# Four rearrangements in a fused state-space and GeGLU kernel: token halves at the start, earlier x, paired gate products, coefficients on GpSimd

## The chip, the cores and the metric

The kernel runs on one core of one Trainium2 chip. The metric is the device time of one execution in microseconds (us). Each change was timed in the same rounds as the kernel before and is given with a 95% interval.

Five engines matter. TensorE (PE in the profile) multiplies matrices, VectorE (DVE) does element-wise work and scans, ScalarE (ACT) does activations and copies, GpSimd (POOL) does small vector work, and SyncE (SP) issues most transfers. The issue queue of SyncE is SPq.

## The reference, cut to what matters

```python
xn = _layernorm(x)                                     # x: [1, 2048, 512]
# A: diagonal complex recurrence, state size 512
h = Lam_bar * h + Bu[t]                                # t = 0 .. 2047, Bu = xn @ B_bar^T
s = 2 * Re(hseq @ Cmat^T) + xn * Dskip
# B: gated feed-forward, F = 1376
g = silu((gelu(xn @ w_gate) * (xn @ w_up)) @ w_down)
out = x + s * g
```

## The kernel before

Tokens are worked in four slabs of 512 (`s`), the 1376 hidden features in eleven tiles (`j`). Per tile, TensorE makes a gate and an up product, ScalarE brings both out of PSUM (gelu, copy), and VectorE multiplies them. The y blocks (output of the recurrence) of slab s-1 are placed between tiles of slab s, and so is the layer norm of slab s+1.

The start normalises slab 0 on VectorE, in two pairs of tiles of 128 tokens, and transposes on TensorE:

```python
dummies(9); ...; dummies(5)               # warm-up matmuls, result unused
...
xs = [norm0(0), norm0(1)]                 # VectorE: xn = (x - mean) * rstd
tps = [t_xn0(0, xs[0]), t_xn0(1, xs[1])]  # TensorE transposes
xnT_out(nc.vector, 0, tps[0])
xnT_out(nc.scalar, 1, tps[1])
xs += [norm0(2), norm0(3)]
second_half()                             # the same for tiles 2 and 3
... # angles: thn, ang, kr on VectorE; sines sh, ch on ScalarE
nc.gpsimd.tensor_copy(out=v4(sa[:]), in_=sh[...])     # wide copy, 128 x 2048
```

The gate and up products of one tile, with the multiplication. `dve(ready, cost, f)` puts an instruction into VectorE's program; a clock of estimated times in the builder decides which waiting instructions go in front of it, so another cost or time changes VectorE's order:

```python
def ffn(s, j, at):
    ... # g_ps = wg tile x xnT, u_ps = wu tile x xnT, 512 columns each
    gt = work.tile([P, TS], BF16, name="gt", tag="gt", bufs=4)
    ACT(out=gt[:fs], in_=g_ps[:fs, :], func=AF.Gelu_apprx_tanh)
    ub = work.tile([P, TS], BF16, name="ub", tag="ub", bufs=4)
    ACT(out=ub[:fs], in_=u_ps[:fs, :], func=AF.Copy)
    dve(now() + 0.9, 0.34, lambda: TT(out=at[:fs, j, :], in0=gt[:fs], in1=ub[:fs], op=ALU.mult))
```

For slabs 2 and 3 the layer norm is made while the slab before is multiplied. ScalarE sums x and its square, seven small operations on GpSimd, one after the other, make the scale `rs` and the bias `nb` of all four tiles, ScalarE normalises, and a transposing transfer from SyncE lays the tile down as `xnT`.

```python
def ln_small(s):
    G = nc.gpsimd
    mean, var = sx[:, s, 0, :], sx[:, s, 1, :]                 # [128, 4] each
    G.tensor_scalar(out=mean, in0=mean, scalar1=1.0 / D, scalar2=None, op0=ALU.mult)
    G.tensor_tensor(out=mq[:, s, :], in0=mean, in1=mean, op=ALU.mult)
    G.tensor_scalar(out=var, in0=var, scalar1=1.0 / D, scalar2=EPS, op0=ALU.mult, op1=ALU.add)
    G.tensor_tensor(out=var, in0=var, in1=mq[:, s, :], op=ALU.subtract)
    G.tensor_tensor(out=rs[:, s, :], in0=var, in1=mhalf[:], op=ALU.pow)
    G.tensor_tensor(out=nb[:, s, :], in0=mean, in1=rs[:, s, :], op=ALU.mult)
    G.tensor_scalar(out=nb[:, s, :], in0=nb[:, s, :], scalar1=-1.0, scalar2=None, op0=ALU.mult)

def ln_out(s, m):
    ACT(out=xn[:], in_=x_tok[:, s * M + m, :], func=AF.Identity, scale=rs[...], bias=nb[...])
    nc.sync.dma_start_transpose(out=xnT[:, :, c0 : c0 + P], in_=xn[:])
```

## Time and profile before

| | before |
|---|---|
| median of the runs | 188.41 us (188.31 to 188.55) |
| span of the profiled core | 186.4 us |
| TensorE busy | 179.5 us, 96% |
| VectorE busy | 155.3 us, 83% |
| GpSimd busy | 16.8 us, 9% |

TensorE sets the time: it is never long without work, and what another engine does counts only where TensorE then waits. A line of the timeline gives start, duration, engine, source line, operation, output<-inputs, shapes and, in brackets, how long the engine had been idle and what released it. For TensorE the bracket counts from the modelled end of the matmul before and comes out about 0.16 us smaller than the delay; a delay of 0.2 us or less shows none. TensorE's timeline, kernel before, at the first product and at the only gap in mid-kernel:

```profile
9.19 1.02 PE L425 MATMUL g_ps<-xnT,wg 128*128 128x512 bf16 x4 [0.69 <-ACT xnT L202]
...
62.97 1.68 PE L460 MATMUL y_ps<-C,hst 128*128 128x512 bf16 x6 [0.50 <-DVE hst L363]
```

The bracket at the y block is that for the first half of hst; with a shorter wait for the second half, inside the group, the block loses 0.89 us.

GpSimd's timeline, kernel before: the wide copy of the start, and the small statistics of slab 2 (made during slab 1):

```profile
10.27 1.89 POOL L245 COPY sa<-sh 128x2048 bf16<-128x2048 bf16 x1 [0.29 <-ACT sh L228]
...
63.62 0.45 POOL L520 TENSOR_SCALAR sx<-sx 128x4 f32<-128x4 f32 x1 [45.96 <-ACT junk L515]
64.15 0.20 POOL L521 TENSOR_TENSOR mq<-sx 128x4 f32<-128x4 f32 x1
64.44 0.20 POOL L522 TENSOR_SCALAR sx<-sx 128x4 f32<-128x4 f32 x1
64.72 0.20 POOL L523 TENSOR_TENSOR sx<-sx,mq 128x4 f32<-128x4 f32 x1
...
67.00 0.28 POOL L526 TENSOR_SCALAR nb<-nb 128x4 f32<-128x4 f32 x1
```

The copy starts after VectorE's normalisation is over (second pair from 7.32 to 8.05 us). The seven small operations take 67.28 - 63.62 = 3.7 us, four of them 0.2 to 0.3 us each. VectorE stands idle during the three of 0.20 us (from 63.99 to 65.30 us), as its timeline of the same kernel shows; whether this is why they are short, e5 bears on below:

```profile
65.30 0.43 DVE L438 TENSOR_TENSOR at<-gt,ub 128x512 bf16<-128x512 bf16 x1 [1.31 <-ACT ub L437]
```

ScalarE needs their result for the four normalisations. The waits of ScalarE, kernel before (total, times, longest):

```profile
ACT xn L530 <- POOL nb L526: 3.8, 2, 2.7
```

### The profile page before, as it was taken

The page shows a single profiled execution, that of the slowest core. Times are in us where ns is not written, and L with a number is a line of the kernel's source. Part 1 is how long each engine was busy: PE and PEld are TensorE (multiplying, and loading weights), DVE is VectorE, ACT ScalarE, POOL GpSimd, SP SyncE. Part 2 cuts the span into 40 slices and gives each one's busy share as a digit, 9 for nine tenths or more (in the row PEclk, how much of TensorE's full clock was granted, in tenths as well). Part 3 has the DMA queues.
Part 4 walks back from the last instruction along what each step waited for, and adds up shares of the span by engine and source line. Part 5 has one row for each costly group of instructions (what it writes and reads, how often), then busy time and mean ns, then how long its engine had stood idle before and what let it go on. Part 6 is the DMA issues. An engine that isn't in the chain of part 4 may idle for free.

```text
span 186.4 us, 2533 instructions
## 1 busy us (share of the span) xinstructions
PE 179.5 (96%) x887; PEld 84.2 (45%) x887; DVE 155.3 (83%) x266; ACT 115.3 (62%) x208; POOL 16.8 (9%) x35
## 2 busy tenths in 40 slices
PE   7699999999999899999999999999999999999992
PEld 2344444444444344544444444544444444554452
DVE  4948999999977799999999999999999999532034
ACT  3289996677799979257259949747428733451210
POOL 3653000000000230000000080000000000000000
PEclk9999999999999999999999999999999999999999
DMA  5994924896000016200000003310000000000001
GB/s 147 336 306 105 223 49 92 221 250 203 0 0 0 0 24 91 58 28 28 0 0 5 2 0 77 91 30 29 0 0 0 0 4 28 28 30 28 32 28 57
DMA packets 24444, 12.26 MB, mean 66 GB/s; under 512 B 15760, under 2 KB 24432, under 8 KB 24432
## 3 DMA queue, kind: packets, MB, share of 16 engines
q1 hardware_dynamic: 24256, 12.03, 25.2%
q8 instruction: 7, 0.11, 0.3%
q10 hardware_dynamic: 176, 0.07, 0.1%
q14 instruction: 5, 0.04, 0.1%
HBM read 6.33 MB, written 2.10 MB: 45 GB/s over the span
## 4 chain that ended last, share of the span: by engine, by line
PE 88%; ACT 5%; DVE 4%; DMA 1%; issue 1%; ACTq 0%
PE f_ps L445 20%; PE g_ps L425 18%; PE up_ps L430 18%; PE u_ps L343 15%; PE y_ps L460 14%; PE y_ps L465 2%; ACT junk L515 1%; DVE st L154 1%; DMA x_tok<-in_A_x_dram 1%; PE y_ps L493 1%; ACT gt L435 1%; ACT ub L437 1%; ACT L435 1%; DVE qq L359 1%; PE tp L174 1%
## 5 line engine op out<-in xcount | busy, mean ns | idle before, releaser
L425 PE MATMUL g_ps<-xnT,wg 128*128 128x512 bf16 (+1 forms) x176 | 45.2, 379 | 0.7 <-ACT xnT L202 0.7
L430 PE MATMUL up_ps<-xnT,wu 128*128 128x512 bf16 (+1 forms) x176 | 45.2, 379 | 0.0
L445 PE MATMUL f_ps<-wd,at 128*128 128x512 bf16 (+1 forms) x176 | 38.7, 379 | 0.0
L435 ACT ACTIVATE gt<-g_ps 128x512 bf16<-128x512 f32 (+1 forms) x44 | 26.4, 600 | 11.1 <-PE g_ps L425 8.6
L389 DVE TENSOR_TENSOR_SCAN Ft<-rho,it,Wt 128x512 bf16<-128x512 f32 x24 | 30.1, 1274 | 0.0
L437 ACT ACTIVATE ub<-up_ps 128x512 bf16<-128x512 f32 (+1 forms) x44 | 26.5, 602 | 5.1 <-PE up_ps L430 4.9
L460 PE MATMUL y_ps<-C,hst 128*128 128x512 bf16 x120 | 28.7, 379 | 0.5 <-DVE hst L363 0.5
L343 PE MATMUL u_ps<-xnT,BT 128*128 128x512 bf16 x128 | 28.4, 379 | 0.0
L430 PEld LDWEIGHTS <-wu 128*128 128x128 bf16 (+1 forms) x176 | 17.6, 100 | 20.4
L445 PEld LDWEIGHTS <-at 128*128 128x128 bf16 (+1 forms) x176 | 17.2, 98 | 20.6
L348 ACT ACTIVATE U<-u_ps 128x512 bf16<-128x512 f32 x32 | 18.9, 610 | 11.1 <-PE u_ps L343 11.1
L425 PEld LDWEIGHTS <-wg 128*128 128x128 bf16 (+1 forms) x176 | 17.1, 100 | 19.0 <-issue 0.8
L438 DVE TENSOR_TENSOR at<-gt,ub 128x512 bf16<-128x512 bf16 (+1 forms) x44 | 18.0, 414 | 7.3 <-ACT ub L437 7.0
L450 ACT ACTIVATE g<-f_ps 128x512 f32<-128x512 f32 x16 | 9.6, 597 | 23.5 <-PE f_ps L445 23.5
L478 DVE TENSOR_TENSOR yg<-y_ps,g 128x512 bf16<-128x512 f32 x15 | 10.3, 684 | 13.7 <-PE y_ps L465 9.9
L343 PEld LDWEIGHTS <-BT 128*128 128x128 bf16 x128 | 12.4, 98 | 14.6
L460 PEld LDWEIGHTS <-hst 128*128 128x128 bf16 x120 | 11.5, 98 | 14.7 <-DVE hst L363 1.5
L530 ACT ACTIVATE xn<-x_tok,nb,rs 128x512 bf16<-128x512 bf16 x12 | 10.0, 832 | 3.8 <-POOL nb L526 3.8
L363 DVE TENSOR_TENSOR hst<-pp,qq 128x1024 bf16<-128x1024 bf16 x16 | 10.6, 688 | 0.2
L363 DVE TENSOR_TENSOR Wt<-pp,qq 128x1024 bf16<-128x1024 bf16 x16 | 10.5, 688 | 0.3
L515 ACT ACTIVATE junk<-x_tok 128x512 bf16<-128x512 bf16 x16 | 10.1, 630 | 0.3
L359 DVE TENSOR_TENSOR pp<-U,cos_b 128x2048 bf16<-128x2048 bf16 x8 | 9.8, 1223 | 0.3
(106 smaller groups left out, 145.0 us busy)
## 6 DMA issues: line engine op xcount, KB each, us to landing
out_dram<-ot SPq DMA_DIRECT2D x15, 128.0 KB, 1.7
x_tok<-in_A_x_dram SPq DMA_DIRECT2D x3, 512.0 KB, 6.9
wd<-in_B_w_down_dram SPq DMA_DIRECT2D x1, 1280.0 KB
wg<-in_B_w_gate_dram SPq DMA_DIRECT2D x1, 640.0 KB, 6.2
wu<-in_B_w_up_dram SPq DMA_DIRECT2D x1, 640.0 KB
wg<-in_B_w_gate_dram SPq DMA_DIRECT2D x1, 384.0 KB, 4.5
wu<-in_B_w_up_dram SPq DMA_DIRECT2D x1, 384.0 KB
wg<-in_B_w_gate_dram SPq DMA_DIRECT2D x1, 352.0 KB
```

The source lines that it names most:

```text
L343: nc.tensor.matmul(u_ps[:, :], lhsT=BT[:, ri, kt, pt * P : (pt + 1) * P], rhs=xnT[:, kt, cols], start=(kt == 0), stop=(kt == KT - 1),)
L348: ACT(out=U[:, ri, q, :], in_=u_ps[:, :], func=AF.Copy)
L363: return lambda: TT(out=dst()[i], in0=box["pp"][:, i, :, :], in1=box["qq"][:, 1 - i, :, :], op=op)
L389: nc.vector.tensor_tensor_scan(out=box["F"][:, ri, q, :], data0=rho[:, pt : pt + 1].to_broadcast([P, TS]), data1=box["W"][:, ri, q, :], in ...
L425: nc.tensor.matmul(g_ps[:fs, :], lhsT=wg[:, kt, fsl], rhs=xnT[:, kt, cols], start=(kt == 0), stop=(kt == KT - 1))
L430: nc.tensor.matmul(u_ps[:fs, :], lhsT=wu[:, kt, fsl], rhs=xnT[:, kt, cols], start=(kt == 0), stop=(kt == KT - 1))
L435: ACT(out=gt[:fs], in_=g_ps[:fs, :], func=AF.Gelu_apprx_tanh)
L437: ACT(out=ub[:fs], in_=u_ps[:fs, :], func=AF.Copy)
L438: dve(now() + 0.9, 0.34, lambda: TT(out=at[:fs, j, :], in0=gt[:fs], in1=ub[:fs], op=ALU.mult))
L445: nc.tensor.matmul(f_ps[:, :], lhsT=at[:fs, k, m0 : m0 + P], rhs=wd[:fs, k, :], start=(k == 0), stop=(k == NFT - 1))
L460: nc.tensor.matmul(y_ps[:, :], lhsT=hst[:, j // NPT, j % NPT, m0 : m0 + P], rhs=C2[:, j // NPT, j % NPT, :], start=(j == 0), stop=False,)
L515: ACT(out=junk[:], in_=x_tok[:, s * M + m, :], func=f, accum_out=sx[:, s, i, m : m + 1])
```

## The change

Four parts, meant to fill TensorE's first microseconds and to relieve VectorE before the first y block:

- **Start.** Gate and up of the first three tiles are made in token halves, so that TensorE can begin when tiles 0 and 1 of x are ready; transposes of tiles 2 and 3 come between the halves, and their normalisation behind the angle steps.
- **x of slab 1** is loaded ahead of the later weights.
- **Pairs.** The gate products of two tiles are multiplied in one VectorE instruction of double length.
- **Coefficients.** Seventeen small operations go from VectorE to GpSimd, four diagonals to ScalarE.

```diff
     load_gu(0)
+    load_x(1)
     load_gu(1)
-    load_x(1)
 ...
+    bn(0, 2)
+    bn(0, 3)
     xs = [norm0(0), norm0(1)]
+    bn_end(0, 2)
+    bn_end(0, 3)
+    rstd(0, 2, 4)
     tps = [t_xn0(0, xs[0]), t_xn0(1, xs[1])]
     xnT_out(nc.vector, 0, tps[0])
     xnT_out(nc.scalar, 1, tps[1])
-    xs += [norm0(2), norm0(3)]
-    second_half()
 ... (angle steps)
     STT(out=kr[:], in0=ang[:], scalar=-1.0, in1=ang[:], op0=ALU.mult, op1=ALU.max)
+    xs += [norm0(2), norm0(3)]
     ACT(out=sh[:], in_=ang[:], func=AF.Sin, scale=TWO_PI)
 ...
-        TT(out=nre[:], in0=rho[:], in1=c1[:], op=ALU.mult)
+        GT(out=nre[:], in0=rho[:], in1=c1[:], op=ALU.mult)     # GT: GpSimd; 16 more like it
 ...
+        if i == 0:
+            pair["g"] = work.tile([P, 2, TS], BF16, name="gt", tag="gt", bufs=2)
+            pair["u"] = work.tile([P, 2, TS], BF16, name="ub", tag="ub", bufs=2)
 ...
-        dve(now() + 0.9, 0.34, lambda: TT(out=at[:fs, j, :], in0=gt[:fs], in1=ub[:fs], op=ALU.mult))
+        elif i:
+            dve(now() + 0.9, 0.61, lambda: TT(out=at[:, j - 1 : j + 1, :], in0=gt[:], in1=ub[:], op=ALU.mult))
 ...
+    for j in range(SPLIT):                                       # SPLIT = 3
+        for up in range(2):
+            early[j, up] = gu_mm(0, j, up, 0, TS // 2)
+        if j == 1:
+            tps += [t_xn0(2, xs[2]), t_xn0(3, xs[3])]
+            xnT_out(nc.vector, 2, tps[2])
+            xnT_out(nc.scalar, 3, tps[3])
 ...
                     fold_c(m)
+                    skip_diag(m)                                 # diagonal, on ScalarE
```

More of the change, by code (lines that the diff above doesn't have):

```diff
@@ L191 @@
     ACT(out=pf[:], in_=pt_ps[:, :], func=AF.Copy)
-    for a in (0, 2):
-        for m in (a, a + 1):
-            bn(0, m)
-        for m in (a, a + 1):
-            bn_end(0, m)
-        rstd(0, a, a + 2)
     def xnT_out(eng, m, tp):
@@ L204, in xnT_out @@
             eng.tensor_copy(out=o, in_=tp[:, :, :])
+    bn(0, 0)
+    bn(0, 1)
+    bn_end(0, 0)
+    bn_end(0, 1)
+    rstd(0, 0, 2)
+    nc.gpsimd.tensor_tensor(out=dt_[:], in0=euler[:], in1=ldt, op=ALU.pow)
+    bn(0, 2)
+    bn(0, 3)
     xs = [norm0(0), norm0(1)]
+    bn_end(0, 2)
+    bn_end(0, 3)
+    rstd(0, 2, 4)
     tps = [t_xn0(0, xs[0]), t_xn0(1, xs[1])]
@@ L209 @@
     xnT_out(nc.scalar, 1, tps[1])
-    xs += [norm0(2), norm0(3)]
-    def second_half():
-        tps.extend([t_xn0(2, xs[2]), t_xn0(3, xs[3])])
-        xnT_out(nc.vector, 2, tps[2])
-        xnT_out(nc.scalar, 3, tps[3])
-    second_half()
-    nc.gpsimd.tensor_tensor(out=dt_[:], in0=euler[:], in1=ldt, op=ALU.pow)
     STT(out=thn[:], in0=lim, scalar=1.0 / (2.0 * math.pi), in1=dt_[:], op0=ALU.mult, op1=ALU.mult)
@@ L251 @@
     diagI = consts.tile([P, KT, P], BF16, name="diagI")
-    def coefficients():
-        nre, nim, den, inv, t1, t2, t3, t4 = (
-            small(n) for n in ("nre", "nim", "den", "inv", "t1", "t2", "t3", "t4")
-        )
-        TT(out=nre[:], in0=rho[:], in1=c1[:], op=ALU.mult)
-        TT(out=nim[:], in0=rho[:], in1=s1[:], op=ALU.mult)
-        TSC(out=nre[:], in0=nre[:], scalar1=-1.0, scalar2=None, op0=ALU.add)
-        TT(out=den[:], in0=lre, in1=lre, op=ALU.mult)
-        TT(out=t1[:], in0=lim, in1=lim, op=ALU.mult)
-        TT(out=t2[:], in0=nim[:], in1=lim, op=ALU.mult)
-        TT(out=t3[:], in0=nim[:], in1=lre, op=ALU.mult)
-        TT(out=den[:], in0=den[:], in1=t1[:], op=ALU.add)
-        TT(out=t1[:], in0=nre[:], in1=lre, op=ALU.mult)
-        TT(out=t4[:], in0=nre[:], in1=lim, op=ALU.mult)
-        nc.vector.reciprocal(out=inv[:], in_=den[:])
-        TT(out=t1[:], in0=t1[:], in1=t2[:], op=ALU.add)
-        TT(out=t3[:], in0=t3[:], in1=t4[:], op=ALU.subtract)
-        TT(out=cre[:], in0=t1[:], in1=inv[:], op=ALU.mult)
-        TT(out=cim[:], in0=t3[:], in1=inv[:], op=ALU.mult)
-        TSC(out=cre[:], in0=cre[:], scalar1=2.0, scalar2=None, op0=ALU.mult)
-        TSC(out=cim[:], in0=cim[:], scalar1=2.0, scalar2=None, op0=ALU.mult)
-        TSC(out=ncre[:], in0=cre[:], scalar1=-1.0, scalar2=None, op0=ALU.mult)
-        for kt in range(KT):
-            TSC(out=diagI[:, kt, :], in0=ident_f[:], scalar1=dsk[:, kt : kt + 1], scalar2=None, op0=ALU.mult)
@@ new lines, with skip_diag @@
+    GT = nc.gpsimd.tensor_tensor
+    GS = nc.gpsimd.tensor_scalar
+    def skip_diag(kt):
+        ACT(out=diagI[:, kt, :], in_=ident_f[:], func=AF.Copy, scale=dsk[:, kt : kt + 1])
+    nre, nim, den, inv, t1, t2, t3, t4 = (
+        small(n) for n in ("nre", "nim", "den", "inv", "t1", "t2", "t3", "t4")
+    )
+    def coefficients():
+        GT(out=nre[:], in0=rho[:], in1=c1[:], op=ALU.mult)
+        GT(out=nim[:], in0=rho[:], in1=s1[:], op=ALU.mult)
+        GS(out=nre[:], in0=nre[:], scalar1=-1.0, scalar2=None, op0=ALU.add)
+        GT(out=den[:], in0=lre, in1=lre, op=ALU.mult)
+        GT(out=t1[:], in0=lim, in1=lim, op=ALU.mult)
+        GT(out=t2[:], in0=nim[:], in1=lim, op=ALU.mult)
+        GT(out=t3[:], in0=nim[:], in1=lre, op=ALU.mult)
+        GT(out=den[:], in0=den[:], in1=t1[:], op=ALU.add)
+        GT(out=t1[:], in0=nre[:], in1=lre, op=ALU.mult)
+        GT(out=t4[:], in0=nre[:], in1=lim, op=ALU.mult)
+        GT(out=t1[:], in0=t1[:], in1=t2[:], op=ALU.add)
+        GT(out=t3[:], in0=t3[:], in1=t4[:], op=ALU.subtract)
@@ L278, in fold_c, with coefficients_end @@
+    def coefficients_end():
+        nc.vector.reciprocal(out=inv[:], in_=den[:])
+        GT(out=cre[:], in0=t1[:], in1=inv[:], op=ALU.mult)
+        GT(out=cim[:], in0=t3[:], in1=inv[:], op=ALU.mult)
+        GS(out=cre[:], in0=cre[:], scalar1=2.0, scalar2=None, op0=ALU.mult)
+        GS(out=cim[:], in0=cim[:], scalar1=2.0, scalar2=None, op0=ALU.mult)
+        GS(out=ncre[:], in0=cre[:], scalar1=-1.0, scalar2=None, op0=ALU.mult)
     def fold_c(pt):
@@ L417, in chain, with gu_mm @@
         )
-    def ffn(s, j, at):
-        cols = slice(s * TS, (s + 1) * TS)
+    SPLIT = 3
+    early = {}
+    pair = {}
+    def gu_mm(s, j, up, a=0, b=TS, ps=None):
         fs = min(P, F - j * P)
         fsl = slice(j * P, j * P + fs)
-        g_ps = psum.tile([P, TS], FP32, name="g_ps", tag="ps")
+        if ps is None:
+            ps = psum.tile([P, TS], FP32, name="up_ps" if up else "g_ps", tag="ps")
+        w = wu if up else wg
         for kt in range(KT):
             nc.tensor.matmul(
-                g_ps[:fs, :], lhsT=wg[:, kt, fsl], rhs=xnT[:, kt, cols], start=(kt == 0), stop=(kt == KT - 1)
-            )
-        u_ps = psum.tile([P, TS], FP32, name="up_ps", tag="ps")
-        for kt in range(KT):
-            nc.tensor.matmul(
-                u_ps[:fs, :], lhsT=wu[:, kt, fsl], rhs=xnT[:, kt, cols], start=(kt == 0), stop=(kt == KT - 1)
-            )
-        pe_takes(2 * KT)
-        gt = work.tile([P, TS], BF16, name="gt", tag="gt", bufs=4)
-        ACT(out=gt[:fs], in_=g_ps[:fs, :], func=AF.Gelu_apprx_tanh)
-        ub = work.tile([P, TS], BF16, name="ub", tag="ub", bufs=4)
-        ACT(out=ub[:fs], in_=u_ps[:fs, :], func=AF.Copy)
-        dve(now() + 0.9, 0.34, lambda: TT(out=at[:fs, j, :], in0=gt[:fs], in1=ub[:fs], op=ALU.mult))
@@ new lines, in gu_mm, with ffn @@
+                ps[:fs, a:b], lhsT=w[:, kt, fsl], rhs=xnT[:, kt, s * TS + a : s * TS + b],
+                start=(kt == 0), stop=(kt == KT - 1),
+            )
+        return ps
+    def ffn(s, j, at):
+        fs = min(P, F - j * P)
+        if s == 0 and j < SPLIT:
+            g_ps, u_ps = (gu_mm(s, j, up, TS // 2, TS, early[j, up]) for up in range(2))
+        else:
+            g_ps, u_ps = gu_mm(s, j, 0), gu_mm(s, j, 1)
+        pe_takes(2 * KT)
+        i = j % 2
+        if i == 0:
+            pair["g"] = work.tile([P, 2, TS], BF16, name="gt", tag="gt", bufs=2)
+            pair["u"] = work.tile([P, 2, TS], BF16, name="ub", tag="ub", bufs=2)
+        gt, ub = pair["g"], pair["u"]
+        ACT(out=gt[:fs, i, :], in_=g_ps[:fs, :], func=AF.Gelu_apprx_tanh)
+        ACT(out=ub[:fs, i, :], in_=u_ps[:fs, :], func=AF.Copy)
+        if j == NFT - 1:
+            dve(now() + 0.9, 0.34, lambda: TT(out=at[:fs, j, :], in0=gt[:fs, 0, :], in1=ub[:fs, 0, :], op=ALU.mult))
+        elif i:
+            dve(now() + 0.9, 0.61, lambda: TT(out=at[:, j - 1 : j + 1, :], in0=gt[:], in1=ub[:], op=ALU.mult))
@@ L532, in ln_out @@
         nc.sync.dma_start_transpose(out=xnT[:, :, c0 : c0 + P], in_=xn[:])
-    clk["pe"] = 9.0
-    clk["dve"] = 10.5
+    for j in range(SPLIT):
[5 more added lines that the diff above has]
+            xnT_out(nc.scalar, 3, tps[3])
+    clk["pe"] = 8.1
+    clk["dve"] = 10.3
     hsts, ats, g2s = {0: hst0}, {0: at0}, {}
@@ L543, in ln1_stats @@
             bn_end(1, m)
-    dve(11.5, 2.8, ln1_stats)
+    dve(10.3, 2.8, ln1_stats)
     G = nc.gpsimd
@@ L562 @@
             if s == 0:
-                if j == 0:
+                if j == 1:
                     ca_wide()
-                if j == 1:
-                    dve(now(), 2.6, coefficients)
+                    coefficients()
+                if j == 8:
+                    coefficients_end()
                 if 3 <= j < 3 + M:
```

## The prediction

> **What bounds the kernel now.** I read the page's busy table first, then the chain of work that ended last, then the timeline of the first 30 us, and last the waits of each engine.
>
> ```profile
> PE 179.5 (96%) x887; PEld 84.2 (45%) x887; DVE 155.3 (83%) x266; ACT 115.3 (62%) x208; POOL 16.8 (9%) x35
> PE 88%; ACT 5%; DVE 4%; DMA 1%; issue 1%; ACTq 0%
> ```
>
> TensorE is busy for 179.5 of 186.4 us and makes up 88% of the chain. It idles for 6.9 us in all; time is to be had there, or in its preparatory work. The timeline places them. Up to 9.19 us PE does warm-up and transposes; the first product starts there. After 183.1 us come the last epilogue and the last store (3.3 us, untouched). Between these there is one gap, near 62 us. The chain in order of time shows both edges that the change can move:
>
> ```profile
> 8.54 0.61 ACT xnT L202
> 9.19 1.02 PE g_ps L425 x4
> ...
> 60.11 0.50 ACT ub L437
> 60.63 0.43 DVE at L438
> 61.05 1.15 DVE qq L359
> 62.22 0.70 DVE hst L363
> 62.97 1.04 PE y_ps L460 x4
> 64.05 0.60 PE y_ps L460 x2
> 64.65 0.22 PE y_ps L465 x4
> 64.88 0.86 PE g_ps L425 x4
> ...
> 68.33 1.73 PE y_ps L460 x8
> 70.06 0.22 PE y_ps L465 x4
> 70.28 0.86 PE g_ps L425 x4
> ```
>
> The first product waits for ScalarE's copy of the fourth transposed tile (8.54 us). The first y block, due when the up product before it ends at 62.04 us (61.01 + 0.17 of fill + 0.86), waits for hst: it ends at 64.88, so it took 2.84 us, where the next one took 70.28 - 68.33 = 1.95. **The stall is worth 0.89 us.** Before it stands VectorE, and before that ScalarE: the products of slab 1 (at) that were queued in front of hst wait for ub.
>
> The timeline shows what feeds these:
>
> ```profile
> 6.08 0.73 DVE L165 TENSOR_SCALAR xn<-x_tok,mv,rs 128x512 bf16<-128x512 bf16 x2
> 7.30 0.60 ACT L202 ACTIVATE xnT<-tp 128x512 bf16<-128x512 bf16 x1 [2.38 <-PE tp L174]
> 12.78 2.47 DVE L154 BATCH_NORM_STATS2 st<-x_tok 128x6 f32<-128x512 bf16 x4 [2.57 <-DMA x_tok<-in_A_x_dram]
> 55.96 0.42 DVE L438 TENSOR_TENSOR at<-gt,ub 128x512 bf16<-128x512 bf16 x1 [1.41 <-ACT ub L437]
> ```
>
> Tiles 0 and 1 of x stand transposed at 7.90 us, 1.3 us before the first product. VectorE waits 2.57 us for x of slab 1.
>
> **What the Trainium skill says.** "VectorE: DVE Perf Modes", section on the TRN2 errata: an operation with an SBUF source pays a fixed latency per instruction whatever its size, measured there as about 150 cycles (about 156 ns at its 0.96 GHz). The trace agrees in these two rows:
>
> ```profile
> L438 DVE TENSOR_TENSOR at<-gt,ub 128x512 bf16<-128x512 bf16 x40 | 16.4, 414 | 6.0 <-ACT ub L437 5.8
> L363 DVE TENSOR_TENSOR hst<-pp,qq 128x1024 bf16<-128x1024 bf16 x16 | 10.6, 688 | 0.2
> ```
>
> Two products of 414 ns against one of double length at 688 ns leaves 140 ns. Neighbours overlap a little, though: the next start follows a 414 ns product after 0.34 us and a 688 ns one after 0.60 us, so a pair gives VectorE only 0.08 us.
>
> "SBUF — State Buffer", "Who interferes with whom", says that a VectorE operation with two SBUF inputs contends with a GpSimd operation that reads SBUF, and whoever came first holds it. The trace fits: the same small product on GpSimd takes 198 ns at 17.1 us and 778 ns in the mean later, beside a full VectorE:
>
> ```profile
> L525 POOL TENSOR_TENSOR nb<-sx,rs 128x4 f32<-128x4 f32 x2 | 1.6, 778 | 0.2
> L550 POOL TENSOR_TENSOR nb<-mv,rs 128x4 f32<-128x4 f32 x1 | 0.2, 198 | 0.1
> ```
>
> "ScalarE: Activation LUTs", "What ACT_TABLE_LOAD costs", gives about 1283 ns for a load; the trace has 1.28 us. Their number does not change. "PSUM — Partial Sum Buffer", "The four PSUM rules": two groups open at once in one bank cannot both clear. Here the first token half is closed before the second opens, so nothing has to be added; no run shows it yet.
>
> **The change, part by part.** *Order of the start.* The statistics of tiles 2 and 3 are still taken before the first normalisation, but their aggregation (0.34 us of VectorE from first start to the next operation) moves behind it. So xn of tile 0 starts at about 5.68 instead of 6.08 us: 0.40 us. ScalarE's copy of tile 1 follows the start of xn 1 by 0.89 us, as before, so it ends at about 7.50 us.
>
> *Token halves.* Gate and up of three tiles, first half: 24 matmuls of 256 columns. The profile has that size in the last block, 8 in 0.87 us, so 0.108 us each, exactly half of 0.216: halving costs PE nothing. First product at about 7.55 us. Tiles 0 and 1 take 16 x 0.108 = 1.73 us, to 9.28. Then PE transposes tiles 2 and 3, 8 in 0.72 us. Are they ready? VectorE copies xnT of tile 0 from about 6.74; the angle steps took 1.96 us from such a copy to the end of kr (8.22 to 10.20, less a short overlap), so xn 2 starts at about 8.7 and xn 3 at 9.03. Transposes: 9.28 to 10.0, about without a gap. Tile 2's halves, 8 x 0.108, to 10.87, cover the copies of tiles 2 and 3 (to 10.15 and 10.7, ScalarE's sines ending at about 9.8). The second halves follow directly. So PE work of 5.18 us (24 x 0.216), which began at 9.19, now begins at 7.55 with 0.72 us of transposes inside: the gain is 9.19 - 7.55 - 0.72 = **0.92 us**. I allow 0.1 for a gap. The schedule's own PE clock, moved from 9.0 to 8.1 by the diff, says the same.
>
> *x of slab 1 first.* 512 KB go ahead of 1280 KB of weights. It landed at about 12.7 us; at the 309 to 314 GB/s that the windows show there it should land at about 8.5 to 9, and the later weights at about 12.7. Tile 3 needs these at 13.5 (gate) and 14.3 (up). VectorE's 2.57 us wait goes, but this alone is not on the PE chain.
>
> *Coefficients.* The 18 small operations and the four diagonals hold VectorE from 16.82 to 19.26, 2.44 us; one reciprocal stays. Seventeen go to GpSimd: at 0.2 to 0.8 us, 3 to 14 us, free until the folding of C at 45 us. Four diagonals go to ScalarE, beside the down products where it had 2.4 us of 10 free; only the last, about 0.25 us, delays slab 1's first gelu.
>
> *Pairs.* Slab 0 saves 5 x 0.08 = 0.4 us of VectorE, the kernel 1.6. The order of instructions shows a larger effect: hst of slab 0 now comes before the first product of slab 1. In the kernel before, three such products stood in front, 3 x 0.34 us and waits of 1.41, 0.24 and 0.77: 3.4 us.
>
> *At the stall.* VectorE is rid of about 2.3 + 0.4 + 3.4 = 6.1 us before hst, which was complete at 63.99: estimate 57.9. PE will want it at 62.04 - 0.9 = 61.1. So the 0.89 us stall goes, with 3 us in hand.
>
> **Sum:** 0.82 + 0.89 = 1.7 us. 188.32 - 1.7 = **186.6 us**.
>
> **The rivals.**
> 1. *A start that jams.* If GpSimd's wide copy of sa (1.89 us, due at about 9.0) holds up xn 3, or sines hold up the copy of tile 3, PE loses up to 1.7 us right where it gains 0.9. For: they now meet in time, which they did not before. Against: xn ran at its usual 0.73 us per two beside GpSimd's pow at 7.32. Total then 187.3 to 188.3 us.
> 2. *Pairs come too late.* With two buffers of two tiles, gelu of tile 4 waits for the product of tiles 0 and 1, in slabs 2 and 3 queued behind a whole chain of rotations. I followed the new order with the old durations: in slab 2 that product ends at about 103.8 us and gelu 4 comes at about 105.6; in slab 3, 142.9 against 145. It fits, by 2 us; an error of 3 us in my VectorE clock would cost about 1 us. Total about 187.5.
> 3. *Only the start gains,* hst being late for another reason (the reciprocal waiting for a GpSimd slowed by the shared port): 187.5 us.
> 4. *Later weights come late:* the first tile 3 product waits up to 1 us: 187.5 us.
>
> **Range and chances.** The PE idle time that the change can reach is 1.64 + 0.89 us, and 0.72 of it is filled by transposes, so below 186 is hardly possible. Each rival costs around 0.9, two of them together about all. I give 0.6 to both gains, 0.3 to one. Range 186.0 to 187.6. Two per cent is 3.8 us: out of reach downwards; upwards it needs a new wait of over 5 us.
>
> **What would show it.** Right: first g_ps at about 7.5 us; PE dense from there, with transposes of tiles 2 and 3 at about 9.3; no wait of y_ps for hst, y blocks of 1.95 us; hst of slab 0 complete near 58; statistics of slab 1 before 11 us without a DMA wait; PE busy still near 179 us, the same matmul work. Wrong: a PE wait for xn or xnT around 10 us; waits of g_ps for a PSUM buffer at 13 to 20 us or in slabs 2 and 3; PE waiting for wg or wu near 13.5 us. A time over 187.6 would mean that one of these is there.

## More of the kernel before

SyncE also issues the stores of the results. In a slab its order is: transpose of tile 0, store of y block 0, transposes of tiles 1 and 2, store of y block 1, transpose of tile 3, further stores.

## The result, and the profile after

| | before | after |
|---|---|---|
| median | 188.41 us (188.31 to 188.55, 4 runs) | 191.18 us (190.93 to 191.4, 4 runs) |
| ratio after / before | | 1.0146, 95% interval 1.0129 to 1.0164 |
| span | 186.4 us | 189.6 us |
| GpSimd busy | 16.8 us | 33.3 us |

Ratios are computed from the mean time of one kernel's fast runs over that of the other's of the same rounds, so they are not quite the ratio of the medians quoted. The change costs 1.5% where 0.9% was to be gained. It stays within 2%, but it is slower, and it lies far above the predicted range. The page of the kernel after, busy times and shares of the chain:

```profile
PE 180.6 (95%) x911; PEld 87.0 (46%) x911; DVE 152.6 (80%) x225; ACT 115.9 (61%) x212; POOL 33.3 (18%) x52
PE 80%; DVE 10%; ACT 6%; DMA 1%; issue 1%; ACTq 0%
```

TensorE's share of the chain fell from 88 to 80%. VectorE and ScalarE now stand in it. Two views of the start say where it begins. TensorE's timeline, kernel after:

```profile
5.25 1.83 PE L146 MATMUL w_ps<-warm 128*128 128x512 bf16 x5
6.91 0.61 PE L174 MATMUL tp<-ident,xn 128*128 128x128 bf16 x8
8.21 0.60 PE L433 MATMUL g_ps<-xnT,wg 128*128 128x256 bf16 x4 [0.69 <-ACT xnT L195]
...
11.60 0.40 PE L174 MATMUL tp<-ident,xn 128*128 128x128 bf16 x4 [1.26 <-DVE xn L165]
```

VectorE and GpSimd in the same microseconds, timeline of the kernel after:

```profile
9.24 2.31 DVE L165 TENSOR_SCALAR xn<-x_tok,mv,rs 128x512 bf16<-128x512 bf16 x2
9.38 2.01 POOL L241 COPY sa<-sh 128x2048 bf16<-128x2048 bf16 x1 [0.29 <-ACT sh L224]
```

The two normalisations took 0.73 us in the kernel before. Now they take 2.31 us and end 0.16 us after GpSimd's copy does, and TensorE waits 1.26 us for the second. That is one part of the loss at the start. The other is 0.66 us of delay of the first product (8.21 us, where 7.55 was predicted): the transposes at 6.91 wait behind the warm-up matmuls, which took 1.83 us for five where the kernel before had 1.25. Ten traces of kernels with the new start agree: the first product comes at 7.65 us where the five took 1.25 us (e8), at 8.09 where they took 1.70 (e6), at 8.44 where they took 2.06 (e3).

The y stall, on the other hand, is gone. VectorE's timeline shows hst, and TensorE's the y block, kernel after:

```profile
56.57 1.29 DVE L366 TENSOR_TENSOR hst<-pp,qq 128x1024 bf16<-128x1024 bf16 x2
...
62.83 1.89 PE L478 MATMUL y_ps<-C,hst 128*128 128x512 bf16 x8
```

hst is complete at 57.86 us, and the y block has no bracket, so no wait. Then new waits follow. GpSimd's timeline, kernel after, for the operations shown above of the kernel before:

```profile
64.86 0.72 POOL L538 TENSOR_SCALAR sx<-sx 128x4 f32<-128x4 f32 x1 [29.67 <-ACT junk L533]
65.66 1.02 POOL L539 TENSOR_TENSOR mq<-sx 128x4 f32<-128x4 f32 x1
66.77 1.09 POOL L540 TENSOR_SCALAR sx<-sx 128x4 f32<-128x4 f32 x1
67.95 0.57 POOL L541 TENSOR_TENSOR sx<-sx,mq 128x4 f32<-128x4 f32 x1
...
70.79 1.12 POOL L544 TENSOR_SCALAR nb<-nb 128x4 f32<-128x4 f32 x1
```

The same seven operations take 71.91 - 64.86 = 7.05 us. Their end is 4.63 us later than before: 3.4 us because they are longer, and 1.24 us because they start later, behind ScalarE's last sum (64.81 instead of 63.57 us). TensorE's later start accounts for most of that, and the y stall, which used to hold TensorE back meanwhile, is gone. VectorE no longer idles there. It has scans in front of it that used to come later; its timeline, kernel after:

```profile
65.42 2.45 DVE L392 TENSOR_TENSOR_SCAN Ft<-rho,it,Wt 128x512 bf16<-128x512 f32 x2
```

ScalarE waits for the last of the seven, and TensorE for ScalarE. ScalarE's and TensorE's timelines, kernel after:

```profile
71.94 0.81 ACT L548 ACTIVATE xn<-x_tok,nb,rs 128x512 bf16<-128x512 bf16 x1 [4.46 <-POOL nb L544]
...
73.29 1.02 PE L433 MATMUL g_ps<-xnT,wg 128*128 128x512 bf16 x4 [1.22 <-ACT gt L451]
...
81.51 7.07 PE L346 MATMUL u_ps<-xnT,BT 128*128 128x512 bf16 x32 [0.70 <-DVE at L456]
```

While ScalarE stands at xn for 4.46 us, the gelus behind it in its program do not run, PSUM fills, and TensorE stops at 73.29. The second stop, at 81.51, opens the next slab's input products, which need the four tiles of xnT. The profile names VectorE as the releaser, which is inferred; the issue queue suggests another. VectorE, ScalarE and SyncE's queue, timeline of the kernel after:

```profile
76.94 0.84 ACT L548 ACTIVATE xn<-x_tok,nb,rs 128x512 bf16<-128x512 bf16 x1
...
77.89 0.43 DVE L497 TENSOR_TENSOR ot<-yg,x_tok 128x512 bf16<-128x512 bf16 x1
...
78.35 0.36 SPq L500 DMA_DIRECT2D out_dram<-ot  x1
78.80 1.19 SPq L550 DMA_TRANSPOSE xnT<-xn  x1
```

The fourth tile was normalised at 77.78, but its transposing transfer stands behind a store whose data (ot) VectorE finishes at 78.32. It goes out at 78.80; at the next slab's start such a transfer took 2.48 us in the chain, which would make it land at about 81.3 (estimate), close to the 81.51 at which TensorE resumes.

The chain dates the same places in both kernels (it counts a group of matmuls from the end of the one before, some 0.16 us later than the timeline; for the 64.94, where the chain after does not pass TensorE, 0.16 is added to the timeline's 64.78). Each row is a place; the last column is what this stretch added:

| place in TensorE's program | before | after | added since the row above |
|---|---|---|---|
| gate of tile 3, slab 0 | 14.53 | 15.49 | +0.96 (start) |
| gate after the first y block, slab 1 | 64.88 | 64.94 | -0.89 (y stall gone) |
| first down product, slab 1 | 86.27 | 88.57 | +1.38 (at 73.29), +0.87 (at 81.51) |
| first down product, slab 2 | 129.48 | 132.26 | +0.47 (transfers, at 125.19) |

The sum is 0.96 - 0.89 + 1.38 + 0.87 + 0.47 = 2.79 us, against 191.18 - 188.41 = 2.77. For TensorE's program the ledger is closed. The match to 0.02 us is partly luck, for these are two single profiles: their spans differ by 3.2 us (the last store, issued 2.8 us later, takes 0.4 us longer), and the kernel before was profiled with an early start (9.19 us; b1 and b2 below, which do not change the start, have 9.35 and 9.44), so some 0.2 us of the 0.96 may be scatter. What stands behind each entry had to be tested.

### The profile page after: what moved, and what is told of

Same layout as the page of the kernel before. It is cut to its first block, busy times and chain, and to the rows that moved or that the text cites. A ratio compares the mean times of both kernels' runs of the same rounds, so it can differ in the third digit from the quotient of the medians.

```text
span 189.6 us, 2535 instructions
## 1 busy us (share of the span) xinstructions
PE 180.6 (95%) x911; PEld 87.0 (46%) x911; DVE 152.6 (80%) x225; ACT 115.9 (61%) x212; POOL 33.3 (18%) x52
## 4 chain that ended last, share of the span: by engine, by line
PE 80%; DVE 10%; ACT 6%; DMA 1%; issue 1%; ACTq 0%
PE f_ps L463 20%; PE g_ps L433 15%; PE up_ps L433 15%; PE u_ps L346 15%; PE y_ps L478 9%; PE w_ps L146 3%; DVE Ft L392 3%; ACT junk L533 2%; ACT gt L451 2%; ACT ub L452 2%; DVE at L456 1%; DMA xnT<-xn 1%; PE y_ps L483 1%; DVE xn L165 1%; PE y_ps L511 1%
## 5 line engine op out<-in xcount | busy, mean ns | idle before, releaser
L433 PE MATMUL g_ps<-xnT,wg 128*128 128x512 bf16 (+2 forms) x188 | 45.7, 365 | 1.9 <-ACT gt L451 1.2
L433 PE MATMUL up_ps<-xnT,wu 128*128 128x512 bf16 (+2 forms) x188 | 45.7, 365 | 0.0
L392 DVE TENSOR_TENSOR_SCAN Ft<-rho,it,Wt 128x512 bf16<-128x512 f32 x24 | 29.2, 1267 | 0.0
L433 PEld LDWEIGHTS <-wu 128*128 128x128 bf16 (+1 forms) x188 | 18.8, 100 | 19.2
L433 PEld LDWEIGHTS <-wg 128*128 128x128 bf16 (+1 forms) x188 | 18.3, 100 | 19.2 <-issue 2.3
L456 DVE TENSOR_TENSOR at<-gt,ub 128x1024 bf16<-128x1024 bf16 x20 | 13.7, 686 | 12.9 <-ACT ub L452 12.8
L478 PEld LDWEIGHTS <-hst 128*128 128x128 bf16 x120 | 11.7, 98 | 13.6
L538 POOL TENSOR_SCALAR sx<-sx 128x4 f32<-128x4 f32 x2 | 1.4, 696 | 66.6 <-ACT junk L533 66.6
```

The source lines that it names most:

```text
L392: nc.vector.tensor_tensor_scan(out=box["F"][:, ri, q, :], data0=rho[:, pt : pt + 1].to_broadcast([P, TS]), data1=box["W"][:, ri, q, :], in ...
L433: nc.tensor.matmul(ps[:fs, a:b], lhsT=w[:, kt, fsl], rhs=xnT[:, kt, s * TS + a : s * TS + b], start=(kt == 0), stop=(kt == KT - 1),)
L456: dve(now() + 0.9, 0.61, lambda: TT(out=at[:, j - 1 : j + 1, :], in0=gt[:], in1=ub[:], op=ALU.mult))
L478: nc.tensor.matmul(y_ps[:, :], lhsT=hst[:, j // NPT, j % NPT, m0 : m0 + P], rhs=C2[:, j // NPT, j % NPT, :], start=(j == 0), stop=False,)
```

## The experiments

Theory, as it stood after the result: **GpSimd and VectorE block each other.** The wide copy holds VectorE at the start, and a VectorE without pauses holds the seven small operations in slabs 1 and 2; late xnT tiles follow from that and from the order of SyncE's queue. Rivals: the start is late only because of the clock or the order of work; the slab stalls come from the pairs' buffers, or from VectorE itself being late.

| run | median us | ratio to before | 95% interval |
|---|---|---|---|
| the changed kernel | 191.18 | 1.0146 | 1.0129 to 1.0164 |
| e1_norms_first | 190.28 | 1.0092 | 1.0077 to 1.0107 |
| e2_sa_on_scalar | 189.79 | 1.0066 | 1.0048 to 1.0085 |
| e3_five_small_ops | 188.75 | 1.0008 | 0.9991 to 1.0024 |
| e4_stats_on_vector | 192.66 | 1.0230 | 1.0197 to 1.0263 |
| e5_single_products | 189.44 | 1.0041 | 1.0023 to 1.0060 |
| e6_stores_after | 190.08 | 1.0078 | 1.0058 to 1.0098 |
| e7_stats_vector_stores_after | 190.04 | 1.0083 | 1.0058 to 1.0109 |
| **e8_scalar_sa_five_ops** | **187.13** | **0.9920** | 0.9901 to 0.9939 |
| b1_pairs_only | 187.82 | 0.9960 | 0.9943 to 0.9976 |
| b2_coefficients_only | 188.76 | 1.0012 | 0.9997 to 1.0026 |
| b4_start_only | 188.05 | 0.9978 | 0.9954 to 1.0001 |
| e11_fewer_dummies | 188.13 | 0.9977 | 0.9941 to 1.0013 |

The runs named e start from the changed kernel, those named b from the kernel before. Medians of the kernel before in these rounds were 188.46 to 188.72 us. All results were correct.

### e1: the second normalisations ahead of the angle steps

```diff
     xnT_out(nc.scalar, 1, tps[1])
+    xs += [norm0(2), norm0(3)]
     STT(out=thn[:], ...)
 ...
-    xs += [norm0(2), norm0(3)]
     ACT(out=sh[:], in_=ang[:], func=AF.Sin, scale=TWO_PI)
```

> Changed kernel, with the normalisation of tiles 2 and 3 moved ahead of the angle steps, so that it ends before GpSimd's wide copy of sa can start. Port theory (sa's copy holds the SBUF port that the second normalisation needs): the two normalisations take 0.73 us again instead of 2.31, the 1.3 us wait of the transposes goes, tile 3's gate starts near 14.4 us instead of 15.3; the time falls by about 1.0 us to 190.2; the stalls of slabs 1 and 2 stay. Rival (the normalisation is late because of its operand from GpSimd): it waits as long as before and the time stays at 191.2.

Measured 190.28 us. The pair is back to its old length, and tile 3's gate starts at 14.38 instead of 15.49 us. VectorE's timeline, e1:

```profile
7.71 0.74 DVE L165 TENSOR_SCALAR xn<-x_tok,mv,rs 128x512 bf16<-128x512 bf16 x2 [0.48 <-POOL rs L161]
```

Of these 1.11 us, 0.54 come from the first product, which this profile has at 7.67 us (five warm-up matmuls in 1.25 us). TensorE then waits 0.70 us for a late copy of xnT at 11.60: on ScalarE it stands behind the sines, and these wait for the angle steps, which now come later. The stalls in slabs 1 and 2 remain (1.21, 0.73 and 0.33 us). So part of the loss is the meeting of normalisation and copy, and moving one away in time removes it, but the old order has a price too.

### e2: the wide copy on ScalarE

```diff
-    nc.gpsimd.tensor_copy(out=v4(sa[:]), in_=sh[:, :, NB : NB + NA].unsqueeze(3).to_broadcast(W4))
 ...
     def ca_wide():
+        ACT(out=v4(sa[:]), in_=sh[:, :, NB : NB + NA].unsqueeze(3).to_broadcast(W4), func=AF.Copy)
```

> Changed kernel, with the wide copy of sa on ScalarE beside that of ca, so that GpSimd does nothing wide. Port theory: the two normalisations take 0.73 us where they are, the transposes' wait of 1.3 us goes, the time falls by about 1.3 us to 189.9. Rival: the normalisations stay at 2.3 us, and the 1.9 us more on ScalarE make the first gelus late, 191.2 or more.

Measured 189.79 us. VectorE's timeline, e2:

```profile
9.33 0.73 DVE L165 TENSOR_SCALAR xn<-x_tok,mv,rs 128x512 bf16<-128x512 bf16 x2
```

The pair stays where the change put it, and the copy alone is gone from beside it: 2.31 becomes 0.73 us. TensorE's transposes follow without a gap, and tile 3's gate starts at 14.14 us although this run began as late as the changed kernel's (first product at 8.30). This settles the 1.26 us wait at the start: it is GpSimd's copy. The stalls in slabs 1 and 2 are as they were (1.21, 0.72 and 0.31 us), although TensorE is there 1.3 us earlier, so they do not come from the start.

### e3: five small operations instead of seven

The scales go into ScalarE's sums (-1/D for the mean, D to the power -0.5 before the square), so that two multiplications fall away.

```diff
-        for i, f in enumerate((AF.Copy, AF.Square)):
+        for i, (f, k) in enumerate(((AF.Copy, -1.0 / D), (AF.Square, D ** -0.5))):
 ...
+        nmean, var = sx[:, s, 0, :], sx[:, s, 1, :]
+        G.tensor_tensor(out=mq[:, s, :], in0=nmean, in1=nmean, op=ALU.mult)
+        G.tensor_tensor(out=var, in0=var, in1=mq[:, s, :], op=ALU.subtract)
+        G.tensor_scalar(out=var, in0=var, scalar1=EPS, scalar2=None, op0=ALU.add)
+        G.tensor_tensor(out=rs[:, s, :], in0=var, in1=mhalf[:], op=ALU.pow)
+        G.tensor_tensor(out=nb[:, s, :], in0=nmean, in1=rs[:, s, :], op=ALU.mult)
-        ... (the seven shown above)
```

> Changed kernel, with the small statistics of slabs 2 and 3 in five GpSimd operations instead of seven (the division by 512 and the sign go into ScalarE's scales). Port theory (each small operation waits out one VectorE operation, about 1.05 us): nb is there about 2.1 us earlier, ScalarE's waits for it fall from 4.5 and 4.2 to about 2.4 and 2.1 us, PE's wait in slab 1 for gelu falls by at least 1 us, the late transposes' waits shrink; the time falls by 1.5 to 2.5 us to about 189.2. Rival (the statistics are late because ScalarE ends them late): nb comes at most 0.4 us earlier and the time stays within 0.5 us of 191.2.

Measured 188.75 us: 1.4% better than the changed kernel. The waits of ScalarE for nb, in the kernel after and then in e3:

```profile
ACT xn L548 <- POOL nb L544: 8.6, 2, 4.5
```

```profile
ACT xn L546 <- POOL nb L542: 4.6, 2, 2.4
```

The longest wait fell from 4.5 to 2.4 us, and no wait of TensorE is marked in slabs 1 and 2, neither for gelu nor for the transfers (about 0.2 us are left at slab 2's start, where the input products at 122.91 follow the group before by 0.43 instead of 0.22 us). Earlier statistics thus remove all three slab entries (1.38, 0.87 and 0.47), nearly to the last; e6 shows what else the last two need. The start was untouched, and its 2.30 us pair is still there.

### e4: six of the seven statistics on VectorE

```diff
     def ln_small(s):
-        G = nc.gpsimd
+        G = nc.vector
 ...
-        G.tensor_tensor(out=rs[:, s, :], in0=var, in1=mhalf[:], op=ALU.pow)
+        nc.gpsimd.tensor_tensor(out=rs[:, s, :], in0=var, in1=mhalf[:], op=ALU.pow)
```

> Changed kernel, with six of the seven small statistics operations on VectorE, in its order where they are issued, and only the power on GpSimd. Port theory: nb is ready about 2 us after the last sum (near 67.5 us instead of 71.9), at the price of about 2.5 us of VectorE time in slab 1, which has slack; the waits of PE in slabs 1 and 2 go; time about 188.7. Rival (ScalarE's late sums are the cause): nb hardly earlier, and VectorE, 2.5 us later in each of two slabs, makes it slower than 191.2.

A miss: 192.66 us, slower than the change itself. The bias was done at 67.05 us, as expected, and the gelu stall is gone. But in VectorE's program the small operations wait for GpSimd's pow, and all that follows waits with them, about 2.5 us. The results ot came later, with them the stores, and behind these the transposing transfers. TensorE's timeline, e4:

```profile
80.57 7.07 PE L346 MATMUL u_ps<-xnT,BT 128*128 128x512 bf16 x32 [1.62 <-DMA xnT<-xn]
```

In slab 2 this wait is 2.16 us. On SyncE's queue a store went out at 77.39 and the fourth transpose directly behind it at 77.84. Here xn was early, and the transfer late all the same, so the order of the queue is a cause of its own. e6 takes this up.

### e5: the pairing undone

The two tiles, instructions and buffers of `ffn` as in the kernel before; all else as changed.

> Changed kernel with the pairing of products undone (one product per tile again, four single buffers), all else as changed. If it is the pairing that made VectorE dense while GpSimd works on the statistics (a pair waits for its second tile, and what stood between moved together): VectorE idles between 63 and 70 us as before, some of the seven GpSimd operations take 0.2 us again, nb comes 1 to 2.5 us earlier, and the time falls by 1 to 2 us to about 189.7, with the start's loss of 1 us left. Rival (taking the coefficients off VectorE is enough to make it dense there): nb as late as now, time 191.2 to 191.6.

Measured 189.44 us, 1.0% better than the changed kernel. With single products VectorE waits for ScalarE again between them (0.77 us up to 64.18 and 0.70 us up to 66.51), and its scans start at 66.90 instead of 65.42. The seven operations, from 64.84 on, take 0.45, 0.49, 0.20, 0.20, 1.04, 0.55 and 0.32 us and end at 68.58 instead of 71.91; two of 0.20 us stand at the second gap. So the pairs hurt, and the traces fit that they do it by closing VectorE's gaps and bringing its scans forward, not by coming late. Waits of 0.30 and 0.28 us for xnT stay at the two slab starts.

### e6: two stores behind the transposes

```diff
-        nc.sync.dma_start(out=out_td[mg : mg + P, :], in_=ot[:])
+        store = lambda: nc.sync.dma_start(out=out_td[mg : mg + P, :], in_=ot[:])
+        held.append(store) if hold else store()      # hold: first two y blocks of slabs 0 and 1
 ...
+                if j == 9:                            # the fourth transpose is issued at j == 8
+                    while held:
+                        held.pop(0)()
```

> Changed kernel; the stores of the first two y tiles of slabs 0 and 1 are issued after the four transposing transfers of the next slab instead of between them. If PE's waits of 0.87 and 0.47 us before the u products (slabs 1 and 2) come from a transfer held on the issuing queue behind a store whose data VectorE has not made: both waits shrink to under 0.4 in sum and the time falls by about 0.9 us to 190.3; the 1.4 us wait for gelu in slab 1 stays. Rival (those waits are for the last normalisation itself, late on ScalarE): less than 0.3 us gained.

Measured 190.08 us; by the ratios 1.0146 - 1.0078 = 0.7%, or 1.3 us, better than the changed kernel, as much as the entries 0.87 + 0.47 = 1.34 together. TensorE's waits at both slab starts are gone. The stop for gelu stays, and a new wait of 0.18 us for yg comes at 86.90. TensorE's timeline of e6:

```profile
73.16 1.02 PE L433 MATMUL g_ps<-xnT,wg 128*128 128x512 bf16 x4 [1.21 <-ACT gt L451]
```

So the wait at 81.51, which the profile had put down to VectorE's at, was the transfer held on the queue: nothing of at was changed here.

### e7: e4 and e6 together

> The run with the small statistics on VectorE (192.66 us, where nb was early and PE yet waited 1.62 and 2.16 us for transposed x), now with the stores behind the transposing transfers as well. If the held queue is what spoiled it, both waits go and the time falls by over 3 us, to about 189.2: the start's loss of about 1 us, less the 0.9 gained at the first y block, and a little. Rival (VectorE itself became the bound): it stays above 191.5.

Measured 190.04 us, by the ratios 1.0230 - 1.0083 = 1.5%, or 2.8 us, less than e4: the queue was what made e4 slow. It is not the 189.2 that I had expected, because TensorE now waits 0.24 us (at 86.00) and 1.19 us (at 128.09) for VectorE's yg, which frees the PSUM buffers of y. VectorE, which now carries the statistics, is late with yg; that the statistics alone made it late was not tested.

### e8: both conflicts removed (e2 and e3)

> Changed kernel with both mendings that each gained alone: the wide copy of sa on ScalarE, and five small GpSimd operations instead of seven. If they are two independent losses, the gains of 1.4 and 2.4 us add up: 187.4 us, under the kernel before by 1.0. If they share a cause or one was masked by the other, 188 or more.

**Measured 187.13 us, ratio 0.992: faster than both kernels.** Page and chain of e8:

```profile
PE 178.7 (97%) x895; PEld 86.7 (47%) x911; DVE 151.2 (82%) x225; ACT 117.7 (64%) x213; POOL 24.0 (13%) x47
...
61.03 1.73 PE y_ps L478 x8
62.76 0.22 PE y_ps L483 x4
```

From 7.65 us on the timeline of TensorE's whole span has no bracket; about 0.2 us of pause remain at slab 2's start, as in e3. Tile 3's gate starts at 13.53 us in the chain (before 14.53, after 15.49), the y block takes 1.95 us, and the span is 184.7 us. Applied to the before median of the first rounds, 0.992 x 188.41 = 186.9 us.

### b1, b2, b4: each part alone on the kernel before

These ask which part brings the conflict. b1 has the pairs alone; b2 the coefficients on GpSimd and the diagonals on ScalarE alone; b4 the whole new start with x of slab 1 first, but single products and coefficients on VectorE. The edits are the pieces of the diff above.

> Kernel before with one part of the change alone: the products of two tiles in one step. If the pairs are what makes VectorE dense beside GpSimd's statistics: the seven small operations in slab 1 take over 5 us instead of 3.7, ScalarE waits over 3 us for nb there, PE waits in slab 1 for gelu or for transposed x, and the time rises by 0.7 to 2 us (189.1 to 190.5). Rival (it needs the coefficients' removal too): within 0.4 us of before, GpSimd as quick as before.

> Kernel before with the coefficients on GpSimd and the diagonals on ScalarE, alone. VectorE is rid of 2.3 us before hst, so the 0.89 us stall of the first y block should go or shrink under 0.3; the start is as before. Time 187.4 to 187.8. Rival (this part feeds the contention in slab 1): nb late by over 1 us, and 188.5 or more.

> Kernel before with the new start alone: token halves, its order, x of slab 1 first; single products, coefficients on VectorE. Port theory: the normalisations collide with sa (2.3 us), tile 3's gate starts about 1 us later than before (15.5 instead of 14.5). At the first y block, where before waits 0.89 us for hst, the later PE hides part of it: a net loss of 0.2 to 1.0 us, 188.7 to 189.5. Rival (the start is sound and only the rest lost time): 187.6.

All three missed, and taught most. b1 is faster (187.82 us), b2 the same (188.76), b4 slightly faster or the same (188.05, its interval just reaches 1). In **every one of them** the y stall is gone: the y block runs from the end of the up product without a wait. The 0.89 us are one gain, which any of the parts takes alone; they do not take it three times.

In b1 the small statistics did suffer. GpSimd's timeline, b1:

```profile
63.77 1.25 POOL L528 TENSOR_SCALAR sx<-sx 128x4 f32<-128x4 f32 x1 [45.86 <-ACT junk L523]
65.11 0.62 POOL L529 TENSOR_TENSOR mq<-sx 128x4 f32<-128x4 f32 x1
```

They took 4.9 us in place of 3.7, and nb came at 68.66, yet TensorE has no bracket afterwards. It starts the two slabs only 0.17 and 0.19 us late (the input products at 78.63 and 122.03 follow the group before by 0.39 and 0.41 instead of 0.22 us): the slack was about of this size, and used up. In b2 nb came at 67.85, and the slab starts waited a little. TensorE's timeline, b2:

```profile
79.08 7.07 PE L350 MATMUL u_ps<-xnT,BT 128*128 128x512 bf16 x32 [0.36 <-DMA xnT<-xn]
...
122.64 7.07 PE L350 MATMUL u_ps<-xnT,BT 128*128 128x512 bf16 x32 [0.19 <-DMA xnT<-xn]
```

These waits (in full 0.53 and 0.35 us: the input products follow by 0.75 and 0.57 us), and a start 0.25 us later in this run, give the gain of the y block back. In b4 the jam at the start is there in full. TensorE's timeline, b4:

```profile
11.61 0.40 PE L174 MATMUL tp<-ident,xn 128*128 128x128 bf16 x4 [1.25 <-DVE xn L165]
```

Tile 3's gate is at 15.50 us, +0.97, and the y stall that goes, -0.89, hides nearly all of it in the total. A run's time alone would have acquitted the new start.

By ratio the three change the time by -0.40, +0.12 and -0.22%, in sum -0.5%. Together they cost +1.46%. Yet each of the three counts the same 0.89 us (0.47%). An estimate that counts them once makes the start and the coefficients together -0.22 + 0.12 + 0.47 = +0.37%, and e5, which is just these two parts without the pairs, measured +0.41%: these two add up. It is the pairs that do not: alone they cost next to nothing by the same count (-0.40 + 0.47), on top of the other two they cost 1.0%. The reading is that each part takes slack away (VectorE's idle gaps, in which GpSimd could work) until none is left; the pairs with only one of the other parts were not run.

### e11: e8 with two warm-up matmuls instead of five

```diff
-    dummies(5)
+    dummies(2)
```

> The better kernel (sa's copy on ScalarE, five small operations) with two warm-up matmuls instead of five after the parameters' transpose. In the traces of the changed kernels the second group ends between 6.5 and 7.3 us and the first transposes start right after it, though xn is there at about 6.2: if that queueing is real, the first gate starts at 7.65 us or just before in the profile, and the runs spread less; the time 186.9 to 187.1. Rival (the clock then rises later and the early matmuls run slow): slower than 187.3.

This was to win the fractions of a microsecond by which the first transposes wait behind the second group of warm-up matmuls. A miss: 188.13 us, and by the ratios 0.6% slower than e8. The four runs fall into two pairs: 187.39 and 187.59 us at a granted clock of 1.0, 188.67 and 188.75 at 0.988. The profile is of a run of the second kind, and there the rival was right. The clock row of its page and, below it, that of e8, then TensorE's timeline, e11:

```profile
PEclk9879999999999999999999999999999999999998
...
PEclk9999999999999999999999999999999999999999
...
8.43 1.06 PE L433 MATMUL up_ps<-xnT,wu 128*128 128x256 bf16 x4
```

The granted clock was 0.57 from 8 to 12 us (1.00 in e8). Four half products take 1.06 us in place of 0.60, until about 11.7 us, and tile 3's gate comes at 15.33 us instead of 13.53. So the warm-up matmuls are no idle ballast here: with three fewer, two executions of four show a lower clock. Why the two at full clock (0.994 and 0.995 of the kernel before) also came out behind e8 is open; no trace of one was kept. As the first transposes come behind the warm-up, whose length varies, the first product starts anywhere from 7.65 to 8.44 us, which is why one profile of the start is not enough.

## Why the prediction was wrong, and where it was right

**Right.** *Halving costs TensorE nothing:* four half products follow each other every 0.43 us, so 0.108 us each, as worked out. *The start, when nothing jams:* in e8 the first product is at 7.65 us (predicted 7.55), the transposes of tiles 2 and 3 run without a gap at 9.43 (predicted 9.28), and tile 3's gate is 1.00 us earlier than before (predicted 0.82 to 0.92). That the size fits so well is luck in part: this profile had a short warm-up (in e2, without the jam too, the first product came at 8.30 and the gate only 0.39 us earlier), and the transposes took 0.45 us where 0.72 were counted. *The y stall:* hst complete at 57.86 us (predicted 57.9), and 0.89 us gained. *x of slab 1:* its statistics ran at 11.80 without a wait for the transfer, but it landed later than the 8.5 to 9 us predicted: in e8, where VectorE was free earlier, they waited for it until 10.43. *The same matmul work:* TensorE is busy 178.7 us in e8; the changed kernel's 180.6 is 1.1 us above the 179.5 of before, and its longer warm-up matmuls can account for it (1.83 against 1.25 us for five, and 4.02 against 3.42 for the nine before). The sum of the gains was sound too: with both conflicts removed the kernel comes to 0.992 of before, about 186.9 us, against 186.6 predicted.

From the 186.6 us predicted to the 191.18 measured are 4.6 us. The start gives some 1.8 of it (+0.96 where -0.82 was forecast), the slabs 2.7 (1.38 + 0.87 + 0.47), for which the prediction's sum has no term at all.

**Wrong, first step: the start has no gap but "0.1".** This is the prediction's rival 1, down to its place ("GpSimd's wide copy of sa ... holds up xn 3"). It was given little weight because a normalisation ran at its usual speed beside a pow on GpSimd. That was the wrong comparison: a pow on 128 x 4 elements is not a copy of 128 x 2048. The second normalisation took 1984 instead of 410 ns, in the view of line L165 of the kernel after (minimum, median, maximum):

```profile
L165 DVE TENSOR_SCALAR xn<-x_tok,mv,rs x4: 400/410/1984, 5.8 to 9.6; 128x512 bf16<-128x512 bf16 x4
```

With the late end of the warm-up, -0.82 became +0.96. e2 and b4 show the copy's share. The share of the warm-up is read from the traces (8.21 us here, 7.65 in e8); e11, which was to test it, changed the clock as well.

**Wrong, second step: GpSimd was priced for the coefficients alone.** The prediction knew that a small product on GpSimd takes 198 ns in one place and 778 ns beside a full VectorE, from two rows of the trace (at the first, VectorE was not idle but at its small operations of 0.15 us each). It used this for the seventeen operations that were moved, which have time until 45 us, and found them free; that was right (the last ended at 35.2 us), though single ones took up to 1.21 us, not 0.8. It did not ask about the seven that were there already, on a path with a few microseconds of slack. A change that takes VectorE's idle time away takes it from GpSimd too. From 3.7 to 7.05 us for the seven, ScalarE's wait of 4.46 us and TensorE's stop follow: +1.38. That this lateness stops TensorE is shown by e3; e5 shows that the closed gaps matter.

**Wrong, third step: transfers were not looked at beyond the first loads.** Transposes of xn stand in SyncE's queue behind stores which wait for VectorE. This had slack in the kernel before, and with late xn it costs 0.87 and 0.47. e6 shows that without this order the late xn costs nothing at the slab starts, and e4 that with it even an early xn comes late.

**Rivals 2, 3 and 4.** Pairs that come late through their buffers (rival 2) did not appear: TensorE's stop at 73.29 waits for a gelu that itself stood behind xn. hst was on time (3), and no product waited for later weights (4).

**Still open.** Which single VectorE instruction holds which GpSimd operation is not in the trace; only the lengths and the coincidence are. Why the pow did not hold the normalisation up is also open, and so is why the same five warm-up matmuls took 1.25 us in one trace and 2.06 in another, the granted clock being 1.00 in both.

## What to carry to other kernels

Work that is moved off a busy engine fills its gaps, and another engine may have lived in those gaps: before moving it, list every operation of the engine that shares something with it, not only the moved ones, and price these for a VectorE without pauses. Look for wide GpSimd copies beside VectorE work on the critical path, and for transfers that stand in the same issue queue behind a store whose data come late. Test parts both alone and together, and read the places in the trace, for three parts may each take the same gain alone and a total can hide a loss behind it.

## What the Trainium skill lacked or had wrong

- "SBUF — State Buffer", section "Who interferes with whom": the section does name `tensor_scalar` among the operations that can take the shared pair and then block against GpSimd for the whole instruction; the prediction quoted its rule on two inputs and passed this one by. The runs agree with it: 1984 in place of 410 ns beside the copy. What the section lacks is the price for a string of dependent small operations on GpSimd. In these traces each was lengthened anew: 0.2 us beside an idle VectorE became 1.0 to 1.1 us beside VectorE's scans of 1.2 us each, so seven went from 3.7 to 7.05 us. Nor does it say why a GpSimd pow of 1.07 us (at 7.02 us in the kernel before) left VectorE's normalisation at 0.41 us.
- "DMA: Bandwidth & Descriptors", section "Issuing engines are not separate DMA queues": it says that starting transfers from several engines saves only sequencer time, "which is usually small relative to the DMA itself". In these runs the sequencer's order cost TensorE 0.87 us in the changed kernel and up to 2.16 us in e4, because a ready transfer stood behind a store that waited for its data; e6 gained 1.3 us from the order alone. The section lacks this wait.
